# Cutting the last attention unit in two, in a fused attention and gMLP kernel

## The chip, the cores and the metric

The kernel runs on one core of a Trainium2 chip. The metric is the device time of one execution in microseconds (us). TensorE is called PE here, VectorE DVE, ScalarE ACT, GpSimd POOL and SyncE SP, as in the profile.

## What is computed

A gate mixes two branches over the same input x, which has 2048 rows (S) of 512 columns (D), in bfloat16:

```python
g = _sigmoid((x * gate_w).sum(-1, keepdims=True))
# branch A: 32 heads of 16 columns, one shared K and V
q = (x @ wq).reshape(B, S, H, Dh).transpose(0, 2, 1, 3)
k = x @ wk
v = x @ wv
scores = jnp.einsum('bhqd,bkd->bhqk', q, k) * Dh ** (-0.5)
p = _softmax(scores, axis=-1)
o = jnp.einsum('bhqk,bkd->bhqd', p, v)
a = o.transpose(0, 2, 1, 3).reshape(B, S, H * Dh) @ wo
# branch B: gated MLP with a mixing over the sequence
z = _gelu(jnp.einsum('bsd,df->bsf', x, w_in))          # F = 1376, halves of 688
z1 = z[..., :Fh]
z2 = _layernorm(z[..., Fh:], axis=-1)
gg = jnp.einsum('ts,bsf->btf', w_sp, z2) + b_sp[None, :, None]
b = jnp.einsum('bsf,fd->bsd', z1 * gg, w_out)
return g * a + (1 - g) * b
```

## The kernel before

**Units and blocks.** Attention is cut into 32 units (`NU`). Unit u takes four heads and one chunk of 512 queries: c = u // 8 is the chunk, t = (u % 8) // 2 the tile of the Q projection, e = u % 2 one half of its heads. A unit has 64 blocks: 16 tiles of 128 keys times 4 heads. One block is one score product (`s_mm`), 128 keys by 512 queries, into one of the eight PSUM banks of 512 columns; an exponential of it; and one product with V (`o_mm`, called PV), which adds up in one bank (`BO`) for the whole unit, each head in its own 32 rows.

**Two routes for the exponential.** ACT does it with its activation function (`exp_op`, line 770) in steps of two or three banks: even steps own banks 2, 3 and perhaps 4, odd ones banks 0 and 1 (`EB`). DVE and POOL do other blocks by a polynomial, in batches of four (one key tile, four heads): `d_A` (line 782) reads one or two PSUM banks, of banks 5 and 4 (`DBK`), `d_u` (line 789) squares, and `d_w` (line 795, DVE or POOL) squares again. Bank 4 is shared: at each even ACT step the planner decides who has it. Such blocks need two PV products, and each unit with polynomial blocks two constant terms more (`KTV`, `SVB`).

**The end of a unit.** When all its PV products are done, DVE transposes the bank in 32x32 squares (`t1_op`, line 807), `norm_ops` takes the reciprocal of the row sums (line 820), multiplies it with the gate's factor (line 825) and the result with the outputs (line 830), and a second transpose (`t2_op`, line 838) brings them into the form that the output projection reads (`OT`). For the last unit this is done in two halves of 256 queries, interleaved. Only one unit at a time is in the PV bank.

**Outputs.** An output row block (`t2`) is 128 rows. It takes six sets of products with `w_out` (z1*gg) and four with `wo`, one for each pair of units (jp); a set is four 32-column instructions (`fm`). One evacuation scales the sum by the gate, and one DMA stores it. The last unit ends the fourth pair of row blocks 12 to 15. Row blocks 12 and 13 are made in two steps: `g_part` leaves all but the last pair's share in SBUF, `g_fin` adds it. Row blocks 14 and 15 (`g_out`) keep nine of their ten sets waiting in a PSUM bank, and the tenth waits for the last unit. These groups stand in the queue `tails`, in the order: parts 12 and 13, flag, 14, 15, fin 12, fin 13. All four stores are issued by SP, once the flag (a check that the exponentials are in range) is known.

**The order of work.** All of this is planned while the program is built: `build_kernel` simulates PE, ACT and DVE with fixed costs and writes each engine's instructions in the order found. PE takes, in this order: scores for ACT when its banks are free; scores for DVE; rounds of PV; pieces of the fill queues (`first`, `early`, `qs`, `outs`, `main`, `tails`). On the chip each engine follows its own list, and only semaphores tie them. Limits steer the planner, in `PR`:

- `FLEX`: an even ACT step leaves bank 4 to DVE while DVE's planned backlog (ns) is below it.
- `RMIN`: no new polynomial batch is begun in the current unit when fewer blocks (plus 4) are left.
- `PRESS`: PV rounds become urgent when so few of the 19 buffers for exponentials are free.
- `W_MIN`: below this planned share of PE's time, dummy products are put in.

`RLAST` is the same as RMIN for the last unit.

**The start.** x comes in by four transposing DMAs from SP, in the order of chunks 0, 3, 2, 1 (`XO`). While PE waits it runs 12 warm-up products of 128x512 (`WARM`). Then the queue `first` runs: K for the first 128 keys, Q tile 0, the rest of K of chunk 0, V of chunk 0, and so on. The first scores need K for 128 keys and the whole of Q tile 0.

## Time and profile before

| what | value |
|---|---|
| median of three runs | 730.46 us (730.2 to 732.36) |
| profiled execution | 732.71 us |
| its span, first to last instruction | 730.6 us |
| mean granted PE clock | 0.994 |
| busy in the span | PE 712.7, DVE 704.5, ACT 711.4, POOL 467.0 us |
| ACT exponentials (line 770) | 741 instructions with table load, 686.2 us busy |
| score products | 2048 |

A row of the order in time reads: start, length, engine, line, operation, output <- inputs, shape, count, and in brackets the engine's idle time just before and who ended it. Merged instructions stand in one row with the length of the whole. A row of groups reads: line, engine, operation, shapes, count, then busy us and mean ns of one, then the idle time before them. The mean of a pipelined instruction is longer than its distance from the next one. SPq and ACTq are the issue of DMAs on these engines. In rows of stretches the last three columns are the granted PE clock, the share of the DMA engines, and GB/s.

### The profile page before, as it was taken

How to read it: one execution, taken by the hardware profiler on the slowest of the kernel's cores; microseconds unless marked ns; L12 is line 12 of the kernel's file. 1: busy time of each engine (PE TensorE's matmuls, PEld its weight loads, DVE VectorE, ACT ScalarE, POOL GpSimd, SP SyncE). 2: the span in 40 equal slices, each digit the busy share in tenths (PEclk: the TensorE clock that was granted, in tenths of full speed). 3: DMA queues.
4: the chain of work that ended last, by engine and by line, in shares of the span. 5: the costliest groups of instructions: out<-in, count | busy, mean ns of one | idle time of the engine just before them, and what ended most of it. 6: DMA issues, size and time to landing. Idle time of an engine off the chain costs nothing.

```text
span 730.6 us, 21786 instructions
## 1 busy us (share of the span) xinstructions
PE 712.7 (98%) x9037; PEld 208.4 (29%) x9037; DVE 704.5 (96%) x1035; ACT 711.4 (97%) x760; POOL 467.0 (64%) x437
## 2 busy tenths in 40 slices
PE   8999999999999999999999999999999999999995
PEld 3322333323422223222222322222232222222321
DVE  6799999999999999999999999999999999999994
ACT  5999999999999999999999999999999999999994
POOL 5834667661177777776676777767776567668660
PEclk9999999999999999999999999999999999999997
DMA  8341000000000001400000050000005000000001
GB/s 170 125 96 24 2 2 2 1 3 2 2 2 2 1 2 20 99 23 9 2 1 2 3 117 22 10 2 2 2 7 112 15 17 2 2 2 2 2 2 33
DMA packets 48609, 17.29 MB, mean 24 GB/s; under 512 B 44180, under 2 KB 47992, under 8 KB 48504
## 3 DMA queue, kind: packets, MB, share of 16 engines
q1 hardware_dynamic: 46392, 15.67, 9.3%
q8 instruction: 72, 1.18, 0.7%
q10 hardware_dynamic: 2112, 0.17, 0.2%
q14 instruction: 33, 0.27, 0.1%
HBM read 3.25 MB, written 2.10 MB: 7 GB/s over the span
## 4 chain that ended last, share of the span: by engine, by line
PE 71%; ACT 17%; DVE 6%; issue 5%; DMA 1%; ACTq 0%; DVEq 0%
PE ps L354 71%; ACT P L770 16%; DVE UW L782 2%; DVE UW L789 1%; DMA xT<-in_A_x_dram 1%; ACT z L1327 1%; DVE UW L795 1%; DVE bst L598 0%; ACT z L592 0%; DVE km L453 0%; DVE KA L426 0%; DVE T L807 0%; ACT L592 0%; DVE outsb L697 0%; DVE QA L471 0%
## 5 line engine op out<-in xcount | busy, mean ns | idle before, releaser
L770 ACT ACTIVATE P<-ps 128x1024 bf16<-128x1024 f32 (+1 forms) x741 | 686.2, 1182 | 5.9 <-PE ps L354 5.6
L795 POOL TENSOR_TENSOR UW<-UW 128x512 f16<-128x512 f16 (+1 forms) x281 | 363.5, 1294 | 161.2 <-DVE UW L795 67.3
L782 DVE TENSOR_SCALAR UW<-ps 128x512 f16<-128x512 f32 (+1 forms) x424 | 346.1, 837 | 2.5 <-PE ps L354 1.4
L354 PE MATMUL ps<-QA,KA 32*128 32x512 bf16 x2048 | 312.4, 384 | 6.1 <-ACT P L770 2.9
L354 PE MATMUL ps<-P,V 128*32 128x512 bf16 x1496 | 212.4, 385 | 0.4 <-issue 0.2
L354 PEld LDWEIGHTS ps<-QA,KA 32*128 32x128 bf16 x2048 | 84.7, 91 | 308.6 <-ACT P L770 153.5
L789 DVE TENSOR_TENSOR UW<-UW 128x2048 f16<-128x2048 f16 (+1 forms) x163 | 171.4, 1054 | 0.6
L354 PE MATMUL ps<-UW,VW 128*32 128x512 f16 x552 | 118.8, 384 | 0.0
L354 PE MATMUL ps<-wT,z 128*32 128x512 bf16 (+1 forms) x1536 | 116.2, 366 | 0.0
L795 DVE TENSOR_TENSOR UW<-UW 128x1024 f16<-128x1024 f16 (+5 forms) x167 | 108.0, 661 | 0.2
L354 PE MATMUL ps<-UW,V 128*32 128x512 f16 x552 | 84.2, 384 | 0.2 <-DVE T L807 0.2
L354 PEld LDWEIGHTS ps<-P,V 128*32 128x32 bf16 x1496 | 49.1, 94 | 57.4 <-issue 51.6
L475 POOL TENSOR_TENSOR QSQ<-QA 128x512 bf16<-128x512 bf16 x16 | 28.9, 1806 | 22.9 <-DVE z L612 7.0
L354 PEld LDWEIGHTS ps<-wT,z 128*32 128x32 bf16 x1536 | 27.7, 94 | 42.6 <-issue 42.0
L354 PEld LDWEIGHTS ps<-UW,VW 128*32 128x32 bf16 x552 | 28.1, 94 | 14.9 <-issue 11.6
L354 PE MATMUL ps<-wout,z 128*32 128x512 bf16 x384 | 31.6, 384 | 0.0
L354 PE MATMUL ps<-win,xT 128*32 128x344 bf16 x512 | 30.8, 312 | 0.1
L830 POOL TENSOR_TENSOR Tn<-T,rc 128x512 bf16<-128x512 f32 x15 | 24.6, 1639 | 6.4 <-DVE UW L782 3.1
L807 DVE STREAM_TRANSPOSE T<-ps 128x512 f32<-128x512 f32 (+1 forms) x33 | 22.6, 688 | 4.1 <-PE ps L354 4.1
L354 PE MATMUL ps<-QA,KTV 128*32 128x512 bf16 x128 | 25.0, 384 | 0.0
L354 PE MATMUL ps<-CT,SVB 128*32 128x512 bf16 x128 | 24.6, 384 | 0.0
L354 PEld LDWEIGHTS ps<-UW,V 128*32 128x32 bf16 x552 | 19.9, 94 | 15.5 <-issue 11.5
(116 smaller groups left out, 378.5 us busy)
## 6 DMA issues: line engine op xcount, KB each, us to landing
out_dram<-outsb SPq DMA_DIRECT2D x16, 128.0 KB, 1.7
win<-in_B_w_in_dram SPq DMA_DIRECT2D x1, 1376.0 KB, 6.5
wout<-in_B_w_out_dram SPq DMA_DIRECT2D x1, 640.0 KB, 4.2
wo<-in_A_wo_dram SPq DMA_DIRECT2D x8, 64.0 KB, 2.3
UW<-in_A_wq_dram SPq DMA_DIRECT2D x1, 384.0 KB, 3.8
wT<-in_B_w_sp_dram SPq DMA_TRANSPOSE x16, 4.6
UW<-in_A_wq_dram ACTq DMA_DIRECT2D x1, 128.0 KB, 3.9
wout<-in_B_w_out_dram SPq DMA_DIRECT2D x2, 48.0 KB, 1.7
```

What stands on the lines that cost most here:

```text
L354: return t.matmul(dst, lhsT, rhs, start=start, stop=stop, tile_position=tp)
L475: dq(pl_q, 1050.0, lambda: op("pool", lambda v: v.tensor_tensor(QSQ[:, q % 2, :], QA[:, q % NQ, :], QA[:, q % NQ, :], ALU.mult), r=[("Q", ...
L770: op("act", lambda a: a.activation(P[:, 512 * p0:512 * (p0 + n)], ps[:, 512 * b0:512 * (b0 + n)], ACT.Exp), r=[bkey(b0 + i_) for i_ in ran ...
L782: op("dve", lambda v: v.tensor_scalar(UW[:, 0, s, 512 * i:512 * (i + n)], bank(b, 512 * n), Q_A, Q_AS, ALU.mult, ALU.add), r=[bkey(b + j) ...
L789: op("dve", lambda v: v.tensor_tensor(src, src, src, ALU.mult), r=k, w=k, tag="dTT")
L795: op(eng, lambda v: v.tensor_tensor(UW[:, 1, s, 256 * a:256 * b], src, src, ALU.mult), r=[("U", s, h) for h in range(a // 2, (b + 1) // 2) ...
L807: return lambda: pgx.op("dve", lambda v: v.transpose(T1[:, jj, c0:c1], bank(BO, c1 - c0, c0)), r=[bkey(BO)], w=[("T1", jj, c0)], tag="T1")
L830: pgx.op(eng, lambda v: v.tensor_tensor(tnv[:, pr, j0:j1, b0:b1, :], t1v[:, j0:j1, b0:b1, 0:16], rc[:, j0:j1, b0:b1].unsqueeze(3).broadcas ...
L1327: op("act", lambda a: a.activation(z1f[:, 512 * i0:512 * (i0 + n)], ps[:, 512 * b0:512 * (b0 + n)], ACT.Gelu_apprx_tanh), r=[bkey(b0 + j) ...
```

## The change

The last unit of 512 queries becomes two units of 256 (`NB` = 32 before, `NU` = 33 now; `bu(u)` gives the old number). A block of a half-unit is still 512 columns wide: two neighbouring key tiles of 256 queries each (`kts`), so it takes two score products and two PV products for each one before, each 256 columns wide. A half-unit has 32 blocks, and each has its own transpose, normalisation and back-transpose. The score products of a step are collected and written out together (`s_flush`). `RHALF` and `max` limit the polynomial batches of the half-units.

Row blocks 12 and 13 need only the first half's result. Their `g_fin` groups now use bank 7 (`BM`) and stand ahead of 14 and 15 in `tails`, so their evacuations and stores come during the second half. Row block 14 is evacuated and stored by ACT, 15 by DVE and SP.

At the start, Q tile 0 is made and evacuated in halves (`g_Q0`), into two banks. PE holds the first scores' place when Q tile 0 is due before the next piece would end (`HSL`). The 12 warm-up products of 512 columns become 43 of 128, and their operand's first 128 columns are set first. The memset of `KTV` goes from DVE to POOL, and small DVE instructions are put ahead of the ones that wait for wq. The planner's assumed arrival times change, and it doubles the cost of a head piece before its time 7000 (`COLD`).

While the last unit's PV is on, DVE leaves itself free for a transpose that is due within 150 ns (`TCH`). Four limits change.

```diff
-NU = 32
+NB = 32
+NU = 33
-WARM = 12
+WARM = 43
 RLAST = 16
+RHALF = 16
+TCH = 1
+TBM = True
+COLD = 7000.0
+HSL = 30.0
-PR = dict(... PRESS=5, FLEX=5000.0, RMIN=32, WBL=0.5, W_MIN=0.9, ...)
+PR = dict(... PRESS=6, FLEX=3800.0, RMIN=36, WBL=0.5, W_MIN=0.92, ...)
...
-        op("dve", lambda v: v.memset(CT[:], 1.0 / 64.0), w=["CT"])
+        op("dve", lambda v: v.memset(CT[:, 0:128], 1.0 / 64.0), w=["CT0"])
+        op("dve", lambda v: v.memset(CT[:, 128:512], 1.0 / 64.0), w=["CT"])
...
-        op("dve", lambda v: v.memset(KTV[:], 0.0), w=["KTV"])
...
+        op("pool", lambda v: v.memset(KTV[:], 0.0), w=["KTV"])
...
-            mm(bank(0), CT[:, 0:128], CT[:], True, True, ["CT"], [bkey(0)], tag="warm")
+            mm(bank(0, 128), CT[:, 0:128], CT[:, 0:128], True, True, ["CT0"], [bkey(0)], tag="warm")
...
+        def g_Q0(h, b):
+            def piece(dt):
+                return lambda: fm(b, 256, 0, wqd[:, dt, 0, :], xT[:, dt, 512 * XO[0] + 256 * h:512 * XO[0] + 256 * h + 256], dt == 0, dt == 3,
+                                  ["wqd0"] + xk(XO[0], 256 * h, 256 * h + 256), "Q")
+            def ev():
+                op("dve", lambda v: v.tensor_copy(QA[:, 0, 256 * h:256 * h + 256], bank(b, 256)), r=[bkey(b)], w=[("Q", 0)], tag="Qev")
...
+        def bu(u):
+            return min(u, NB - 1)
+        def kts(u, kt):
+            return (kt,) if u < NB - 1 else (2 * kt, 2 * kt + 1)
...
+        def s_flush():
+            for i in range(2):
+                for b, (u, k, g), key in s_pend:
+                    ks = kts(u, k)
+                    if i >= len(ks):
+                        continue
+                    kt, w = ks[i], 512 // len(ks)
+                    e, q, q0 = bu(u) % 2, (bu(u) // 2) % NQ, 0 if u < NB - 1 else 256 * (u - NB + 1)
+                    kr = ["K0a" if kt == 4 * XO[0] else ("K0", kt // 4)] if e == 0 else [("K1", kt // 4)]
+                    mm(bank(b, w, w * i), KA[32 * g:32 * g + 32, e, 128 * kt:128 * kt + 128], QA[32 * g:32 * g + 32, q, q0:q0 + w], True, True,
+                       kr + [("Q", q)], [key], tp=(32 * g, 0), chan="s", tag="S")
+            s_pend.clear()
...
-            if u == NU - 1:
-                for h in range(2):
-                    dq(t1_q, 370.0, t1_op(pg, u, 256 * h, 256 * h + 256), t, None)
...
+            if u >= NB - 1:
+                h = u - NB + 1
+                dq(t1_q, 370.0, t1_op(pg, u, 256 * h, 256 * h + 256), t, setT(("O", u)))
+                for z in norm_ops(pg, c, jp, [1], 8 * h, 8 * h + 8, [("T1", 1, 256 * h)]):
+                    dq(t1_q, *z, t, None)
+                rk = [("Tn", pr, 0, 0), ("Tn", pr, 1, 8 * h)]
+                dq(t1_q, 370.0, t2_op(pg, c, jp, 256 * h, 256 * h + 256, rk, ("OT", 3, 3, h)), t, setT(("OT", 3, 3, h)))
                 return
...
-        first = deque([g_K(XO[0], 0, 128), g_Q(0, DBK[0]), g_K(XO[0], 128, 512), g_V(XO[0], BO), ...
+        first = deque([g_K(XO[0], 0, 128), g_Q0(0, DBK[0]), g_Q0(1, BO), g_K(XO[0], 128, 512), g_V(XO[0], DBK[0]), ...
...
-        tails = deque([g_part(12), g_part(13), g_flag(),
-                       g_out(14, BM, None, True, "sp"),
-                       g_out(15, DBK[0], lambda: d_done(), True, "sp"),
-                       g_fin(12, EB[0][0], lambda: when(("Bend", 0)), "sp"),
-                       g_fin(13, EB[1][0], lambda: when(("Bend", 1)), "sp")])
+        tail_f = [g_fin(12 + i, BM if TBM else EB[i][0], (lambda: 0.0) if TBM else (lambda i=i: when(("Bend", i))), "sp") for i in range(2)]
+        tail_o = [g_out(14, BM, None, True, "act"), g_out(15, DBK[0], lambda: d_done(), False, "sp")]
+        tails = deque([g_part(12), g_part(13), g_flag()] + (tail_f + tail_o if TBM else tail_o + tail_f))
...
+                c_ = fp[1].pieces[fp[1].pos][0] * (2.0 if now < COLD else 1.0)
+                q0 = T.get(("Q", 0), 0.0)
+                if k == 0 and now < q0 < c_p + c_ - HSL:
+                    return None
...
+            if t1_q and st_["pu"] >= NU - TCH and qt(t1_q[0]) <= now + 150.0:
+                return None
```

## The prediction

> **What bounds the kernel now.** I read the busy shares of the page first, then busy time by stretches, then the groups with shapes kept apart, then the order of time in the first 10 and the last 15 us.

> ```profile
> PE 712.7 (98%) x9037; PEld 208.4 (29%) x9037; DVE 704.5 (96%) x1035; ACT 711.4 (97%) x760; POOL 467.0 (64%) x437
> 600.00:700.00 100.00, 100.00 (x1225) 28.27 (x1223) 99.22 (x134) 100.00 (x110) 70.30 (x60) 1.00 0.01 3
> 710.00:720.00 10.00, 9.78 (x128) 2.86 (x128) 6.07 (x10) 9.43 (x9) 1.46 (x2) 1.00 0.01 2
> ```

> (The columns of the second and third rows are the stretch, its length, then busy us of PE, PEld, DVE, ACT and POOL.) In the body three engines are full at once: 99 to 100 of 100 us. ACT does 110 steps in 100 us, 0.909 us a step. So the body gets shorter only if the split of blocks between ACT and DVE gets better, not by removing a wait. The slack lies at the ends: DVE falls to 6.07 of 10 us before the last exponential has ended, and behind it comes a serial tail.

> ```profile
> 704.08 15.35 ACT L770 ACTIVATE P<-ps 128x1024 bf16<-128x1024 f32 x15
> ...
> 719.48 0.39 PE L354 MATMUL ps<-P,V 128*32 128x512 bf16 x2
> 719.92 0.78 DVE L807 STREAM_TRANSPOSE T<-ps 128x256 f32<-128x256 f32 x2 [3.90 <-PE ps L354]
> ...
> 721.46 0.76 DVE L838 STREAM_TRANSPOSE OT<-Tn 128x256 bf16<-128x256 bf16 x2
> 721.95 1.90 PE L354 MATMUL ps<-wo,OT 128*32 128x512 bf16 x16 [2.07 <-DVE OT L838]
> ...
> 722.62 1.41 DVE L697 SCALAR_TENSOR_TENSOR outsb<-ps,G,z 128x512 bf16<-128x512 f32 x2 [0.40 <-PE ps L354]
> ...
> 723.40 3.18 SPq L662 DMA_DIRECT2D out_dram<-outsb  x4
> 723.47 1.27 ACT L728 ACTIVATE outsb<-ps,G 128x512 bf16<-128x512 f32 x2 [4.04 <-PE ps L354]
> ```
> ```profile
> 724.18 2.39 SPq L662 DMA_DIRECT2D out_dram<-outsb  x3
> ```
> ```profile
> L662 SPq DMA_DIRECT2D out_dram<-outsb x16: 332/338/1202, 311.2 to 726.1; - x16
> ```

> The last exponential ends at 704.08 + 15.35 = 719.43. Then: last products 719.48, transposes, normalisation, back-transposes to 722.22, sixteen products of the output projection, two evacuations on DVE and two on ACT, four stores on one queue, the last of which is issued at 726.1. The span ends at 730.6, 4.5 us behind that issue: 11.2 us with hardly any overlap.

> At the head ACT waits until 9.27:

> ```profile
> 1.44 4.45 PE L353 MATMUL ps<-CT 128*128 128x512 bf16 x12 [1.44 <-DVE CT L254]
> ...
> 6.37 0.41 PE L354 MATMUL ps<-xT,wk_rep 128*32 128x128 bf16 x16 [0.48 <-DMA xT<-in_A_x_dram]
> ...
> 6.59 1.05 PE L354 MATMUL ps<-xT,wqd 128*32 128x512 bf16 x16
> ...
> 7.14 0.29 DVE L426 CAST KA<-ps 128x128 bf16<-128x128 f32 x1 [1.05 <-PE ps L354]
> ...
> 7.69 0.69 DVE L471 CAST QA<-ps 128x512 bf16<-128x512 f32 x1 [0.26 <-PE ps L354]
> ...
> 8.14 0.71 PE L354 MATMUL ps<-wvg,xT 128*32 128x33 bf16 x56
> ...
> 8.78 0.39 PE L354 MATMUL ps<-QA,KA 32*128 32x512 bf16 x4
> ...
> 9.27 5.28 ACT L770 ACTIVATE P<-ps 128x1536 bf16<-128x1536 f32 x5 [5.01 <-PE ps L354]
> ```

> Q is in SBUF at 7.69 + 0.69 = 8.38, but the first scores start at 8.78, since the V products stand before them in PE's order.

> **The tail, costed.** The second half-unit has one transpose, one chain of normalisation and one back-transpose where the pair of halves has two of each:

> ```profile
> L807 DVE STREAM_TRANSPOSE T<-ps 128x256 f32<-128x256 f32 x2 | 0.8, 429 | 3.9 <-PE ps L354 3.9
> L838 DVE STREAM_TRANSPOSE OT<-Tn 128x256 bf16<-128x256 bf16 x2 | 0.8, 419 | 0.0
> L830 DVE TENSOR_TENSOR Tn<-T,rc 128x128 bf16<-128x128 f32 x2 | 0.5, 284 | 0.0
> L820 DVE RECIPROCAL rc<-T 128x8 f32<-128x8 f32 x2 | 0.3, 182 | 0.0
> L825 DVE TENSOR_TENSOR rc<-rc,RT 128x8 f32<-128x8 f32 x2 | 0.3, 148 | 0.0
> ```

> Single durations 429 + 182 + 148 + 284 + 419 ns = 1.46 us. The pair interleaves and hides the hand-off between dependent instructions; a single chain shows it, so I add 0.2 (estimate): T2 ends at 719.92 + 1.66 = 721.6, not 722.22. Then two sets of products instead of four, 721.65 to about 722.4, and two evacuations at once: ACT's (0.69, half of the 1.27 with its start) to 722.9, DVE's (about 0.75) to 723.15. One store goes out on ACT's queue, one on SP's. SP's second store was issued 0.15 after its evacuation (722.62 + 1.41 = 724.03, then 724.18), so its issue now stands at about 723.3 in place of 726.1: **-2.8 us**. In the group rows the longest issue took 1202 ns against a median of 338; if the pair meets that, 0.9 comes back. If the last stores also land sooner because two share the engines instead of four, some 0.3 more is gained. Bounds -3.1 to -1.9.

> The clock has a part in it:

> ```profile
> 722.00:723.00 1.00, 1.00 (x12) 0.41 (x16) 0.60 (x2) 0.00 (x0) 0.00 (x0) 0.50 0.00 0
> ```

> The granted clock is 0.50 there, some two us after PE fell idle. In the changed kernel output products can fill that pause (below), and the last sets then run at full clock; that is in the 722.4.
> [...]

> **What is moved ahead.** Row blocks 12 and 13 need only the first half-unit: two sets of products, two DVE evacuations (1.41 together) and two SP stores now run while the second half computes, as does the first half's chain of 1.46. DVE has room: it stood idle 3.90 us before the final transpose. SP must have seen the flag before its first store; the flag is made ahead of these groups, and nothing else is queued on SP. ACT's store is the last thing on ACT.

> The price is on PE. The groups come from one queue in order, so the nine early sets each of row blocks 14 and 15 now wait until 12 and 13 have begun. Before, they ran here:

> ```profile
> 706.00:708.00 2.00, 0.88 (x12) 0.22 (x12) 0.00 (x0) 1.00 0.00 0
> ...
> 714.00:716.00 2.00, 0.97 (x16) 0.23 (x12) 0.00 (x0) 1.00 0.00 0
> ```

> ```profile
> 712.88 0.39 PE L354 MATMUL ps<-wout,z 128*32 128x512 bf16 x4
> ...
> 713.53 0.61 PE L354 MATMUL ps<-wout,z 128*32 128x512 bf16 x8
> ```

> (First the stretches of PE products that read wout, first and last; then two rows of the order in time.) A set of four takes 0.39 us alone and 0.61 - 0.39 = 0.22 behind another, so 18 sets are 3.9 us. They can start about 5 us before the last exponential ends: the second half has 32 blocks, of which ACT does some 20 (estimate), ten steps or 9 us, and the first half's chain and two BM evacuations take about 4 of them. In those 5 us PE gives perhaps 0.33 us a step, 1.9; the pause after the last PV gives another 1.7. That holds nearly all; I charge **+0.2**, bounds 0 and +1.9 (nine sets uncovered).

> **Cutting the unit.** Scores and PV of its 64 blocks come as 256-wide instructions, twice as many:

> ```profile
> L354 PE MATMUL ps<-wT,z 128*32 128x512 bf16 x1280 | 105.2, 384 | 0.0
> ...
> L354 PE MATMUL ps<-wT,z 128*32 128x256 bf16 x256 | 11.0, 276 | 0.0
> ```

> The 512-wide product takes 384 ns, the 256-wide one 276: 256 columns cost 108, no fixed part shows, so about **+0.1**. One more hand-over of the single PV bank holds PV back for one half transpose, 0.43 and a wait: covered by other products, 0; uncovered it is one ACT step, +0.9.

> **The head.** The Q tile in halves lets DVE start earlier, though two 256-wide evacuations together take more than 0.69; Q is ready at about 8.2 to 8.4. What moves is the order: PE now waits for Q and issues the scores before the V pieces, 8.35 instead of 8.78. **-0.4** for ACT's first step. It is worth nothing if DVE or PE set the next 20 us, -0.6 if all lines up. Warm-up:

> ```profile
> L353 PEld LDWEIGHTS ps<-CT x12: 98/151/151, 1.4 to 5.3; 128*128 128x128 bf16 x12
> ```

> Twelve 512-wide products took 4.45 us from 1.44. Forty-three quarter-wide ones have 43/48 of those columns, 4.0 us, and start some 0.3 earlier: over by 5.2, 1.2 us before x. Were the weight load (151 ns) to pace them, 43 x 0.151 = 6.5 us, ending at 7.6, 1.2 us late. Value 0, bounds 0 and +1.2.
> [...] No run here shows 128-wide warm-ups.

> The KTV memset goes from DVE to POOL:

> ```profile
> 13.07 0.95 POOL L340 MEMSET bspz<- 128x1024 bf16 x1
> ...
> 19.11 0.53 POOL L509 TENSOR_SCALAR VW<-V 128x128 bf16<-128x128 bf16 x1 [1.89 <-DVE gs L495]
> ```

> Twice 1024 elements, so 1.9 us ahead of bspz, and POOL stands idle 1.89 us before 19.11: absorbed, 0. Uncovered, KTV comes up to 1.9 later.

> **The limits.** They reorder everything between. Costs of the two routes:

> ```profile
> L770 ACT ACTIVATE P<-ps 128x1024 bf16<-128x1024 f32 x725 | 668.1, 1175 | 0.5 <-PE ps L354 0.3
> L782 DVE TENSOR_SCALAR UW<-ps 128x512 f16<-128x512 f32 x296 | 191.1, 676 | 1.9 <-PE ps L354 1.2
> L782 DVE TENSOR_SCALAR UW<-ps 128x1024 f16<-128x1024 f32 x128 | 155.0, 1211 | 0.6 <-PE ps L354 0.2
> ```

> A block on ACT costs 0.909/2 = 0.45 us; a DVE batch of four spares ACT 1.8. The 296 + 2 x 128 = 552 blocks are 138 batches. FLEX at 3800 leaves the shared bank to ACT more often, RMIN at 36 stops late batches, PRESS at 6 issues PV rounds sooner, W_MIN adds dummy products. Two batches more would be -3.6, three fewer +5.4. DVE was full in the body before, so no term has a clear sign: value 0, both ends kept.

> Sum: -2.8 + 0.2 + 0.1 - 0.4 = **-2.9**. The profiled execution took 732.71 (span 730.6 and 2.1 around it); the sum would make it 729.8. It stands 2.25 above the median 730.46, so a median is forecast at **727.5**.

> **Rivals.**
> 1. The limits help too: one or two DVE batches more, -1.8 to -3.6 on top: 724 to 725.7. For it: the last fifteen steps took 15.35/15 = 1.02 us against 0.909, 1.7 us lost. Against: DVE is full. 0.25.
> 2. The gain is taken back on PE: 18 sets late (+1.9) or a late warm-up (+1.2): 728.7 to 729.4, no change. 0.15.
> 3. Slower: FLEX takes the shared bank from DVE and its paired first steps break up. A pair costs 1211 ns, two singles 1352, so 141 ns each. With DVE full, its loss is spread over both engines: DVE does 552 of 2048 blocks, 27%, so end time grows by about 0.27 of it, 0.04 a pair; all 128 pairs cost 4.9. Alone it offsets 2.9 only from 76 pairs on, but each DVE batch that the bank no longer feeds adds up to 1.8; with three batches fewer (+5.4): 727.5 + 5.4 = 732.9. 0.12.
> 4. The change does not do what it says: the first half's stores stay at the end, because unit 31's PV is closed only when ACT is nearly done. Then only the head's 0.4 and ACT's own queue are left: 729.5. 0.05.

> My forecast holds 0.43. About 0.3%, 2.2 us, is what a measurement can tell from no change: faster means below 728.3. From the cases: faster 0.68 (forecast and rival 1), same 0.2 (rivals 2 and 4), slower 0.12 (rival 3). The range takes rival 1's far end and rival 3's near one: 723.3 to 732.5; the likeliest case's own range is 726 to 729.

> **What would show it.** Two output stores some 8 us ahead of the end, on SP, and two last ones on two queues less than 4 us after the last PV; the first exponential at about 8.9; the last at about 719; 138 batches give or take two, read from the count of 128x512 products of UW and VW (552); the 18 sets between 714 and 722. Wrong would be a changed count of ACT steps that outweighs the tail, PE products between the last PV and T2 that run past it, or warm-ups that end after x has landed.

## The result, and the profile after

The changed kernel took **732.71 us** (median of 18 runs, 730.72 to 734.48) against 730.32 for the kernel before (18 runs, 729.89 to 732.94): ratio **1.0025, 95% interval 1.0016 to 1.0034**. By the medians it is slower by 2.4 us (the ratio compares the means: 1.8 us), where 3 us less were forecast.

The profiled execution of after took 732.71 us too, with a span of 730.9. The shown execution of before was one of its longer ones, so a second profile of the unchanged kernel was taken (730.16 us, span 728.2, granted clock 0.997), and all comparisons below are with that. First the page's busy line of after, then two stretches of each kernel (columns as in the prediction: stretch, length, busy us of PE, PEld, DVE, ACT, POOL, granted clock, DMA share, GB/s).

```profile
PE 715.8 (98%) x9304; PEld 215.4 (29%) x9304; DVE 704.4 (96%) x1041; ACT 711.1 (97%) x757; POOL 471.8 (65%) x442
```

Kernel before, second profile:

```profile
10.00:30.00 20.00, 18.89 (x440) 7.05 (x428) 14.51 (x32) 19.94 (x22) 14.87 (x31) 1.00 0.60 148
30.00:700.00 670.00, 664.11 (x8213) 191.39 (x8209) 665.08 (x948) 669.02 (x718) 440.28 (x377) 1.00 0.08 18
```

After:

```profile
10.00:30.00 20.00, 17.42 (x384) 6.06 (x380) 12.99 (x25) 16.35 (x17) 13.73 (x26) 0.83 0.65 142
30.00:700.00 670.00, 664.49 (x8304) 191.85 (x8304) 663.29 (x959) 669.53 (x717) 446.99 (x387) 1.00 0.09 18
```

ACT's work is the same (711.1 us against 711.4). The loss is in the first 30 us: ACT was busy 16.35 of 20 us in place of 19.94, and PE's mean clock there was 0.83. The body is full in both (669.53 and 669.02 of 670).

ACT in order of time in that stretch, after:

```profile
9.04 1.94 ACT L811 ACTIVATE P<-ps 128x1536 bf16<-128x1536 f32 x2 [4.77 <-PE ps L363]
12.76 3.28 ACT L811 ACTIVATE P<-ps 128x1536 bf16<-128x1536 f32 x3 [1.78 <-PE ps L363]
16.45 1.02 ACT L811 ACTIVATE P<-ps 128x1024 bf16<-128x1024 f32 x1 [0.41 <-PE ps L363]
18.03 1.02 ACT L811 ACTIVATE P<-ps 128x1024 bf16<-128x1024 f32 x1 [0.56 <-PE ps L363]
19.49 1.02 ACT L811 ACTIVATE P<-ps 128x1024 bf16<-128x1024 f32 x1 [0.43 <-PE ps L363]
20.98 9.63 ACT L811 ACTIVATE P<-ps 128x1024 bf16<-128x1024 f32 x9 [0.47 <-PE ps L363]
```

The first step comes at 9.04, in before's second profile at 9.74: 0.70 won. After two steps ACT waits 1.78 us for scores, then about 0.47 ahead of each of the four rows until 20.98: 1.78 + 0.41 + 0.56 + 0.43 + 0.47 = 3.65 us idle. What PE did meanwhile, in order of time, after:

```profile
1.04 4.77 PE L362 MATMUL ps<-CT 128*128 128x128 bf16 x43 [1.04 <-DVE CT L260]
6.22 0.62 PE L363 MATMUL ps<-xT,wk_rep 128*32 128x128 bf16 x16 [0.41 <-DMA xT<-in_A_x_dram]
6.60 1.27 PE L363 MATMUL ps<-xT,wqd 128*32 128x256 bf16 x32
7.70 0.83 PE L363 MATMUL ps<-xT,wk_rep 128*32 128x384 bf16 x16
8.35 0.27 PE L363 MATMUL ps<-wvg,xT 128*32 128x33 bf16 x16
8.55 0.39 PE L363 MATMUL ps<-QA,KA 32*128 32x512 bf16 x4
8.88 0.54 PE L363 MATMUL ps<-wvg,xT 128*32 128x33 bf16 x48
9.31 1.05 PE L363 MATMUL ps<-xT,wk_rep 128*32 128x512 bf16 x16
10.17 0.46 PE L363 MATMUL ps<-wvg,xT 128*32 128x33 bf16 x31
12.07 0.27 PE L363 MATMUL ps<-wvg,xT 128*32 128x33 bf16 x13 [1.44 <-issue]
```

The warm-ups end at 5.81, before x. Then, in the middle of a run of 44 equal V products, PE stops for 1.44 us with no operand late ("issue": nothing the profile shows was waited for). The counts ahead of the stop add up to 43+16+32+16+16+4+48+16+31 = **222 products**. Before the kernel is over its clock, too, has halved twice; stretches of 3.41 us and what follows them, after:

```profile
10.45:13.86 3.41, 1.65 (x55) 0.70 (x41) 1.16 (x2) 1.63 (x3) 1.72 (x5) 1.00 0.79 157
13.86:20.70 6.84, 6.56 (x45) 1.18 (x45) 4.67 (x10) 5.25 (x6) 6.18 (x10) 0.50 0.81 144
713.61:717.02 3.41, 2.54 (x42) 0.86 (x42) 3.38 (x6) 3.41 (x5) 0.00 (x0) 1.00 0.06 19
717.02:720.42 3.40, 3.40 (x40) 0.96 (x42) 3.40 (x6) 3.14 (x3) 0.00 (x0) 0.50 0.19 65
```

From 13.86 to 20.70 PE is full at half clock and ACT waits for it. The tail, after:

```profile
716.00 11.26 SPq L686 DMA_DIRECT2D out_dram<-outsb  x3
...
719.09 1.45 ACT L811 ACTIVATE P<-ps 128x1536 bf16<-128x1536 f32 x1 [0.26 <-PE ps L363]
...
720.81 1.02 ACT L811 ACTIVATE P<-ps 128x1024 bf16<-128x1024 f32 x1 [0.27 <-PE ps L363]
...
722.11 1.02 ACT L811 ACTIVATE P<-ps 128x1024 bf16<-128x1024 f32 x1 [0.28 <-PE ps L363]
...
723.95 0.45 DVE L849 STREAM_TRANSPOSE T<-ps 128x256 f32<-128x256 f32 x1 [2.71 <-PE ps L363]
...
726.37 0.69 ACT L752 ACTIVATE outsb<-ps,G 128x512 bf16<-128x512 f32 x1 [3.24 <-PE ps L363]
727.09 0.37 ACTq L686 DMA_DIRECT2D out_dram<-outsb  x1
```

Kernel before, second profile:

```profile
717.59 2.05 ACT L770 ACTIVATE P<-ps 128x1024 bf16<-128x1024 f32 x2
...
720.13 0.78 DVE L807 STREAM_TRANSPOSE T<-ps 128x256 f32<-128x256 f32 x2 [3.89 <-PE ps L354]
...
722.16 1.05 PE L354 MATMUL ps<-wo,OT 128*32 128x512 bf16 x16 [2.07 <-DVE OT L838]
...
723.04 1.26 ACT L728 ACTIVATE outsb<-ps,G 128x512 bf16<-128x512 f32 x2 [3.40 <-PE ps L354]
```

Here is a surprise about the forecast's own base. The unchanged kernel's tail, from the last exponential's end (719.64) to the span's end (728.2), is **8.5 us** in this execution, and 11.2 in the one that was shown. There the sixteen output products had taken 1.90 us at half clock (here 1.05), and from the last evacuation's end to the span's end it was 730.6 - 724.74 = 5.9 us (here 728.2 - 724.30 = 3.9). After's tail is 730.9 - 723.13 = 7.8. The whole difference of the two spans, +2.7 us, step by step (after minus before's second profile):

| step | before | after | difference |
|---|---|---|---|
| first exponential | 9.74 | 9.04 | -0.70 |
| ACT idle from there to 30 us | 0.06 | 3.65 | +3.59 |
| ACT idle, 30 to 700 us (670 less busy) | 0.98 | 0.47 | -0.51 |
| ACT idle, 700 us to the last exponential | 0 | 0.26+0.27+0.28 = 0.81 | +0.81 |
| ACT's own work up to the last exponential (rest) | | | +0.30 |
| last exponential's end to the last transpose | 0.49 | 0.82 | +0.33 |
| transpose to the last evacuation's end | 4.17 | 3.11 | -1.06 |
| last evacuation's end to the span's end | 3.90 | 3.84 | -0.06 |
| sum | | | +2.70 |

### The profile page after: what moved, and what is told of

The parts are those of the page before. It is cut to its first block, busy times and chain, and to the rows that moved or that the text cites. A ratio compares the mean times of both kernels' runs of the same rounds, so it can differ in the third digit from the quotient of the medians.

```text
span 730.9 us, 22335 instructions
## 1 busy us (share of the span) xinstructions
PE 715.8 (98%) x9304; PEld 215.4 (29%) x9304; DVE 704.4 (96%) x1041; ACT 711.1 (97%) x757; POOL 471.8 (65%) x442
## 4 chain that ended last, share of the span: by engine, by line
PE 69%; ACT 18%; DVE 8%; issue 4%; DMA 1%; ACTq 0%
PE ps L363 69%; ACT P L811 17%; DVE UW L824 3%; DVE bst L622 2%; DVE UW L831 1%; DMA xT<-in_A_x_dram 1%; DVE UW L837 1%; ACT z L616 0%; DVE KA L435 0%; DVE mv L626 0%; DVE QA L480 0%; ACT L616 0%; DVE T L849 0%; ACTq L161 0%; ACT outsb L752 0%
## 5 line engine op out<-in xcount | busy, mean ns | idle before, releaser
L363 PE MATMUL ps<-QA,KA 32*128 32x512 bf16 (+1 forms) x2112 | 312.2, 379 | 7.0 <-ACT P L811 3.9
L363 PE MATMUL ps<-P,V 128*32 128x512 bf16 (+1 forms) x1540 | 207.3, 381 | 0.0
L363 PE MATMUL ps<-UW,VW 128*32 128x512 f16 (+1 forms) x572 | 119.3, 376 | 0.0
L837 DVE TENSOR_TENSOR UW<-UW 128x1024 f16<-128x1024 f16 (+4 forms) x174 | 107.6, 633 | 0.1
L363 PE MATMUL ps<-UW,V 128*32 128x512 f16 (+1 forms) x572 | 82.2, 379 | 0.0
L484 POOL TENSOR_TENSOR QSQ<-QA 128x512 bf16<-128x512 bf16 x15 | 26.0, 1736 | 9.9 <-DVE UW L837 4.4
L363 PE MATMUL ps<-CT,SVB 128*32 128x512 bf16 (+1 forms) x132 | 24.4, 378 | 0.0
L363 PE MATMUL ps<-QA,KTV 128*32 128x512 bf16 (+1 forms) x132 | 24.0, 377 | 0.0
```

Source lines behind the costliest of these rows:

```text
L363: return t.matmul(dst, lhsT, rhs, start=start, stop=stop, tile_position=tp)
L484: dq(pl_q, 1050.0, lambda: op("pool", lambda v: v.tensor_tensor(QSQ[:, q % 2, :], QA[:, q % NQ, :], QA[:, q % NQ, :], ALU.mult), r=[("Q", ...
L837: op(eng, lambda v: v.tensor_tensor(UW[:, 1, s, 256 * a:256 * b], src, src, ALU.mult), r=[("U", s, h) for h in range(a // 2, (b + 1) // 2) ...
```

## The experiments

Theory A, a guess formed from the stop behind the 222nd product (1.44 us, no operand late) and from the half clock behind it (13.86 to 20.70): PE's instructions come in portions, and the new start uses up a portion before the next has arrived; the idle time then costs the clock. Rivals: B, the warm-ups' shape or their end costs (too cold, too late); C, the four limits made a worse plan; D, the cut of the last unit costs more than it brings.

**1. The old warm-ups in the new kernel.** 12 products of 512 columns.

```diff
-WARM = 43
+WARM = 12
-            mm(bank(0, 128), CT[:, 0:128], CT[:, 0:128], ...)
+            mm(bank(0), CT[:, 0:128], CT[:], ...)
```

> The changed kernel with the old warm-up alone: 12 products of 128x512 and their operand set at once; every other instruction and its order as in the changed kernel. Theory A (PE's instruction stream stalls at its 222nd product, which the 43 small warm-ups and the split Q tile bring too early): the stall of 1.44 us at 10.63 comes 31 products later, behind the first V products of chunk 3, and is shorter; the granted clock stays near 1.0 between 10 and 20 us in place of 0.69; ACT has 9 or more busy us there in place of 6.8; the time is 2 to 4 us below the changed kernel, 728.5 to 730.5. Theory B (the new limits cost the time): no change beyond 0.5 us, 732. Theory C (the end of the kernel costs it, by a clock that falls at 717): no change in the head, 732.

731.9 us (731.14 to 732.99, 8 runs; before 730.16), ratio 1.0027 [1.0016, 1.0037]: above the 728.5 to 730.5 that theory A had expected. PE in order of time around the stop:

```profile
11.27 0.20 PE L362 MATMUL ps<-wvg,xT 128*32 128x33 bf16 x4
13.25 0.23 PE L362 MATMUL ps<-wvg,xT 128*32 128x33 bf16 x8 [1.77 <-issue]
```

The stop has moved to 11.5, other products stand ahead of it, and their count is again 12+16+32+16+16+4+48+16+44+3+8+3+4 = 222. Fewer warm-ups alone don't remove it.

**2. Count against shape.** 10 large warm-ups, then 33 products of one column: 43 instructions, with the warming done by large ones.

```diff
-        for _ in range(WARM):
-            mm(bank(0, 128), CT[:, 0:128], CT[:, 0:128], ...)
+        for _ in range(10):
+            mm(bank(0), CT[:, 0:128], CT[:], ...)
+        for _ in range(33):
+            mm(ps[0:1, 0:1], CT[:, 0:1], CT[:, 0:1], ...)
```

> The changed kernel with 10 warm-up products of 128x512 and 33 of a single column: as many products as the 43, but the warming done by large ones. Theory A: the stall stands at the same product, the 222nd, and the time stays at 732 to 733.5. Rival D (not the count but the small products' weaker warming lets the clock fall): the clock holds through 10 to 20 us and the time falls to 729 to 730.5 as with the old warm-up.

732.74 us (730.24 to 735.56, 12 runs), ratio 1.0035 [1.002, 1.0051]: as slow as after. The stop, 1.90 us, again ends ahead of the 223rd product, at 12.94. The shape of the warm-ups (B) falls as the cause; the number of instructions matters. These warm-ups end at 6.8, later than the 5.81 of after, and the first step comes at 9.45; an end that is too late is answered by after itself, where the warm-ups end 0.41 us before the first products on x.

**3. The many warm-ups in the kernel before.** Nothing else changed but their operand, whose first 128 columns are set first.

```diff
-WARM = 12
+WARM = 43
-            mm(bank(0), CT[:, 0:128], CT[:], ...)
+            mm(bank(0, 128), CT[:, 0:128], CT[:, 0:128], ...)
```

> The kernel before with the new warm-up alone: 43 products of 128x128, the first 128 columns of their operand set first; all else as before. Theory A: its 222nd product comes 31 products earlier, among the V products of chunk 3 or the K products ahead of them; a stall of 1 us or more stands at 10 to 12 us where 0.68 us stood at 13.4; the granted clock falls in the 10 us behind it in some or all executions; 731.5 to 734. Theory B and C: 730.3, within 0.5.

733.64 us (731.84 to 734.09, 5 runs), ratio 1.0039 [1.0026, 1.0052]: this line of the change by itself loses 3.5 us.

```profile
14.04 0.35 PE L355 MATMUL ps<-wvg,xT 128*32 128x33 bf16 x22 [1.69 <-issue]
```

The kernel before has its own small stop of 0.57 us ahead of the 223rd product (start to start, at 14.04), nearly all covered by work that ACT has; 31 more instructions ahead of it make it 1.69.

**4. A quarter of the instructions.** K, V and the first Q tile of the start are written as four 32-column products each. Here each four are one 128-column product with the same result; with 12 large warm-ups, all else as in after.

```diff
+        def fw(b, n, off, lhsT, rhs, start, stop, r, tag):
+            mm(ps[:, 512 * b + off:512 * b + off + n], lhsT, rhs, start, stop, r, [bkey(b)], tag=tag)
...
-                return lambda: fm(b, 256, 0, wqd[:, dt, 0, :], ...
+                return lambda: fw(b, 256, 0, wqd[:, dt, 0, :], ...
```

(and the same in `g_K` and `g_V`)

> The changed kernel with 12 large warm-ups, and the K, V and first Q products of the start as one 128-column product each in place of four of 32 columns: the same sums in the same order with a quarter of PE's instructions there. Theory A: PE reaches its 222nd product past 18 us instead of 11.5, the stall is gone or falls where it is covered, the clock holds, the first step comes at 8.6 or earlier, and the time is 726 to 728.5. If the single products cost more than the stall (weight loads of 128 columns, or a change of tiling between them and the score products): 730 or above.

**728.77 us** (727.82 to 733.59, 12 runs; before 730.28, 23 runs), ratio 0.999 [0.9973, 1.0007]. ACT in order of time, then 20 us of the stretches:

```profile
9.01 17.56 ACT L813 ACTIVATE P<-ps 128x1536 bf16<-128x1536 f32 x17 [4.75 <-PE ps L362]
```
```profile
10.00:30.00 20.00, 18.84 (x256) 6.74 (x254) 14.18 (x31) 19.89 (x22) 17.30 (x35) 1.00 0.53 143
```

Seventeen exponentials run on end, with no stop; PE issues 256 products in these 20 us in place of before's 440. The profiled execution has a span of 726.7. Eight of the twelve runs took 727.8 to 729.0 at a granted clock of 0.997 or more, four 730.2 to 733.6 at 0.988 to 0.994. So with the start mended the rest of the change seems worth about 1.5 us where the clock holds. Over all twelve runs no gain is shown: the interval holds 1.

**5. The same in the kernel before.** K and V of the start wide.

> The kernel before with its K and V products of the start as one 128-column product each in place of four. Theory A: its stall of 0.6 us goes, ACT's idle time to 30 us was only 0.3 us, so at most 0.5 us is gained: 729.5 to 730.3. If wide products cost by themselves: 731 or above, and the same amount has to be taken off the result of the changed kernel with wide products.

732.97 us (730.72 to 734.37, 12 runs), ratio 1.0028 [1.0016, 1.0041]: worse, although no stop is left. (About 1 us of it lies outside the span: in the median run the time exceeds the span by 3 us here and by 2 in the kernel before.)

```profile
9.65:13.06 3.41, 2.50 (x29) 0.94 (x26) 1.38 (x7) 3.35 (x4) 2.54 (x7) 1.00 1.13 238
13.06:19.88 6.82, 6.82 (x36) 1.08 (x33) 4.71 (x7) 5.58 (x6) 3.54 (x7) 0.50 0.75 233
```

PE was busy 2.50 of 3.41 us from 9.65 on, and the clock halved for 6.82 us behind it. So the clock halved here without the stop, as it did in after behind a stretch of 3.41 us in which PE was busy 1.65: of theory A, this run shows the second half without the first.

**6. Only K and Q wide.** V stays in four, to keep PE busier; 12 large warm-ups.

> The changed kernel with 12 large warm-up products, and with the K and first-Q products of the start as one 128-column product each; V stays in four 32-column products. Theory A (PE's instructions arrive late at a fixed count, the 222nd): K and Q lose 3 of 4 instructions, so the count is reached about 1.5 us later than in the run with large warm-ups alone (13.25) but earlier than with V wide too; the pause is shorter than 1 us, and more of it is covered by work that ACT already has; time 728 to 730. Theory B (the wide products make PE idle more and so lose the clock): V in four keeps PE busier between 8 and 20 us, the clock holds in more executions than with all three wide, and the time is 727.5 to 728.5. Rival (neither, only the number of warm-up instructions counts): as with 12 large warm-ups alone, 731.9.

732.42 us (730.22 to 735.2, 12 runs; before 730.45), ratio 1.0024 [1.0011, 1.0038]. I expected 727.5 to 730; the miss shows most. No stop at the 222nd product, which comes only at 16.7. But later, PE in order of time and then ACT:

```profile
20.27 0.59 PE L362 MATMUL ps<-V,KN 128*32 128x32 bf16 x56
22.37 0.22 PE L362 MATMUL ps<-V,KN 128*32 128x32 bf16 x4 [1.51 <-issue]
```
```profile
23.62 1.02 ACT L813 ACTIVATE P<-ps 128x1024 bf16<-128x1024 f32 x1 [1.47 <-PE ps L362]
```

A stop of 1.51 us, ahead of the 348th product (counted in the trace), 125 behind the 223rd, inside another run of small products. The clock had halved at 21.42 already, inside the stop, behind a stretch (18.01 to 21.42) in which PE was busy 2.43 of 3.41 us, and it stayed so until 28.24. So the 222nd product is no oddity of its place: a stop of the same kind, 1.51 us with no operand late, stands some 125 products behind it too.

**7. Every product of that kind wide, through the whole kernel.**

> The changed kernel with 12 large warm-up products and with every full-width product (K, V, Q, PV, output projection) of the whole kernel as one 128-column instruction instead of four of 32 columns: a quarter of the instructions for these through the whole span. Theory A (instruction supply matters at the start alone): the head as with K, V and Q wide, no pause at the 222nd product; in the body nothing changes, since PE is bound by columns there: 727.5 to 729.5. Theory C (fewer instructions free PE's sequencer in the body as well): below 727. Rival D (four 32-column products run side by side on PE's column groups and hand over without a gap, one wide product does not, or the clock falls): 731 or more, with PE's idle time in the body above that of the kernel before.

737.28 us (735.05 to 740.05, 6 runs), ratio 1.0099 [1.0072, 1.0125]. The head is as in 4 (first exponential 8.70, no idle to 26 us), so the loss lies behind:

```profile
710.00:720.00 10.00, 8.28 (x145) 3.37 (x141) 8.91 (x15) 9.90 (x11) 1.66 (x2) 0.89 0.05 16
```

PE paused (8.28 of 10), the mean clock fell to 0.89, and the last exponential ended at 726.8. The row holds little of the loss: ACT was idle for 2.35 us between 30 and 700 us and 2.38 from 700 us to the last exponential (0.82 and 0 in experiment 4), and its own work up to there took 713.3 us in place of 708.7. Why was not taken apart. A quarter of the instructions helped at the start alone (728.77 us in experiment 4).

**8. The limits.** The four old limits in the changed kernel:

```diff
-PRESS=6, FLEX=3800.0, RMIN=36, WBL=0.5, W_MIN=0.92
+PRESS=5, FLEX=5000.0, RMIN=32, WBL=0.5, W_MIN=0.9
```

> The changed kernel with the four old limits. Theory A: the head is planned nearly the same, the stall and the low clock stay, 731 to 733. Theory B: the time falls by 2 us or more, below 730.5.

736.9 us (733.71 to 737.34, 6 runs), ratio 1.0083 [1.0068, 1.0098], which neither theory had expected. The reverse, the four new limits alone in the kernel before:

> The kernel before with the four new limits alone. The changed kernel lost 4.2 us when they were set back, so if they are better by themselves: 726 to 729. If they only suit the cut unit or the new start (the planner's order changes as a whole with each): 730 to 734.

735.2 us (734.83 to 737.66, 6 runs), ratio 1.0071 [1.0056, 1.0086]. C falls as a cause of the loss, and the limits are no gain of their own either: +4.9 us in the kernel before, -4.2 in the changed one.

**9. The whole old start** (order, warm-ups, Q in one piece, memsets) with the cut unit and the new limits:

```diff
-        first = deque([g_K(XO[0], 0, 128), g_Q0(0, DBK[0]), g_Q0(1, BO), g_K(XO[0], 128, 512), ...
+        first = deque([g_K(XO[0], 0, 128), g_Q(0, DBK[0]), g_K(XO[0], 128, 512), ...
-COLD = 7000.0
-HSL = 30.0
+COLD = 0.0
+HSL = 1e9
...
```

> The changed kernel with the whole start as before: 12 large warm-ups, one Q tile, the old places of the memsets and small DVE instructions, the old assumed times. The cut unit, its early stores and the new limits stay. Theory A (the start costs what the end gains): stall of about 0.6 us at the 222nd product, ACT idle below 1 us from its first step to 30 us, first step at 9.3, last at about 719.5, then 7.8 us: a span of 725 to 727.5 and a time of 727 to 729, faster than before by 0.2 to 0.45%. Theory B (the new limits or the cut cost it): 730 or above even so.

738.42 us (736.55 to 739.2, 4 runs), ratio 1.0113 [1.0099, 1.0128]: a wide miss. Order of time:

```profile
712.67 0.43 DVE L848 STREAM_TRANSPOSE T<-ps 128x256 f32<-128x256 f32 x1
...
720.69 0.74 DVE L707 TENSOR_SCALAR z<-ps,G 128x512 f32<-128x512 f32 x1
721.85 0.45 DVE L848 STREAM_TRANSPOSE T<-ps 128x256 f32<-128x256 f32 x1 [0.41 <-PE ps L362]
...
723.47 0.10 DVE L777 CAST flag<-ps 1x1 int32<-1x1 f32 x1
...
724.86 6.95 SPq L685 DMA_DIRECT2D out_dram<-outsb  x3
```

The first half's transpose is as early as in after (712.67; 712.48 there), and the second half's comes 0.9 us behind the last exponential (720.95). What is late is the queue `tails`: the part of row block 13 is evacuated only at 720.69 (709.21 in after) and the flag is known only at 723.47 (714.08 in after). All that stands behind it in the queue comes then, the first half's stores too, and the last evacuation starts at 730.70. The stores stay at the end, as in the prediction's rival 4, but not for the reason that it gave (a late end of the first half). Why PE left these pieces so late under the new limits is not shown.

**10. The cut alone:** 9 with the old limits as well.

> The cut of the last unit and the early stores alone: the start and the four limits are those of the kernel before, so only the tail's part of the change is left (the order of the whole kernel is still planned anew). Theory A (the tail's step is a gain by itself, the rest of the loss came from the start): last exponential to end 7.8 to 8.6 us, the last exponential at 718.5 to 719.7 as before, 47 blocks begun by 30 us, time 726.5 to 728. Theory B (every new plan costs, unless its limits are chosen for it): the last exponential ends at 721 or later, or unit 31 closes late and the distance to the end is 13 us, as in the run with the start of before and the new limits (738.42): 732 to 739. Theory C (the tail gives nothing by itself): 730 to 731.

730.82 us (median of 10 runs; nine took 730.33 to 733.04, one 1949.23), before 730.07, ratio 1.001 [0.9999, 1.0021]. Order of time:

```profile
719.91 0.69 DVE L836 TENSOR_TENSOR UW<-UW 128x1024 f16<-128x1024 f16 x1
...
721.10 0.45 DVE L848 STREAM_TRANSPOSE T<-ps 128x256 f32<-128x256 f32 x1 [0.49 <-PE ps L362]
...
723.69 0.69 ACT L751 ACTIVATE outsb<-ps,G 128x512 bf16<-128x512 f32 x1 [4.41 <-PE ps L362]
```

The stores of row blocks 12 and 13 are early, transpose to last evacuation takes 724.38 - 721.10 = 3.28 us in place of 4.17, and the clock holds to the end (1.0 over the span). But the last exponential ended at 719.28 and the transpose waits until 721.10 for a DVE batch that is multiplied until 720.60: 1.8 us in place of 0.5. The gain is eaten by the late batch. Here, then, it is the place of the last batch that is late; in 9 it was the output pieces. (D: no loss of its own is shown, and no gain.)

The runs with the start and the limits set apart, medians:

| | old limits | new limits |
|---|---|---|
| start of before, unit whole | 730.3 | 735.2 |
| start of before, unit cut | 730.8 | 738.4 |
| new start, unit cut | 736.9 | 732.7 |
| new start with wide products, unit cut | | 728.8 |

**11. The kernel before again**, for the second profile used above.

> The kernel before, unchanged, for a second profile of it. Theory (the shown profile was one of its longer executions, its body is the same each time): span 727.6 to 729 at a granted clock of about 0.997, the 222nd product of PE again behind a pause of 0.5 to 0.7 us that ends at 14.0 +- 0.2, and a distance from the last exponential's end to the span's end below 11.2, by up to 2 us, since less of it runs at half clock. Rival (the longer time came from the body): the last exponential ends 2 us earlier than 719.4 and the tail stays at 11.2.

730.16 us, span 728.2; last exponential at 719.64, tail 8.5, half clock in its last 4.3 us. The rival falls: the body was the same, the shown execution's excess lay in the tail, 2.2 us of it behind the issue of the last store.

## Why the prediction was wrong

**The head, -0.4: the step that failed.** The prediction ordered PE's products by their operands alone: "PE now waits for Q and issues the scores before the V pieces, 8.35 instead of 8.78. -0.4 for ACT's first step". That much came true: scores at 8.55, and the first step 0.70 earlier than in the second profile of the kernel before (0.23 earlier than in the shown one). What it did not ask is whether PE can stop with no operand late, as it did for 1.44 us in after. In the kernel before, the small stop stood in the order of time of the shown execution:

```profile
14.04 0.39 PE L354 MATMUL ps<-P,V 128*32 128x512 bf16 x2 [0.19 <-issue]
...
14.82 9.70 ACT L770 ACTIVATE P<-ps 128x1024 bf16<-128x1024 f32 x10 [0.27 <-PE ps L354]
```

The 223rd product starts here, and ACT waits 0.27 us behind it: a sign that was passed over. The new start sends products faster: 43 warm-ups for 12, 32 Q products for 16, and small V products early. The price was 3.59 us of ACT idle time, 1.78 in the stop and 0.41 to 0.56 ahead of each of four steps at half clock. Bounds of -0.6 to 0 held nothing of it.

**Warm-up, 0, bounds 0 and +1.2.** The forecast "over by 5.2, 1.2 us before x" had the side of x right: they ended at 5.81, 0.41 before the first products on x (6.22). They took 4.77 us, not 4.0, which cost nothing. The sixteen first K products took 0.62 us, 0.41 in the shown execution of the kernel before. But its second profile has 0.59 there, and the changed kernel with the old limits (experiment 8), with the same 43 warm-ups, 0.41; so this differs between executions and not by the warm-ups alone. The cost, 3.5 us by itself in the kernel before (experiment 3), went with the count of instructions (experiment 2: as many of another shape, 732.74 us), for which the sum had no term.

**The tail, -2.8: the last issue moved nearly as forecast, the end did not follow it as far.** The stores of row blocks 12 and 13 did go out in the second half (SP's first at 716.00), the 18 sets did fit, T1 to the end of T2 took 725.65 - 723.95 = 1.70 us for a forecast 1.66. "Its issue now stands at about 723.3 in place of 726.1" is 3.9 us behind the last exponential in place of 6.7; after has 727.09 - 723.13 = 4.0. In before's second profile it is 725.9 - 719.6 = 6.2 (the row gives shortest, median and longest issue in ns, then the first and last start):

```profile
L662 SPq DMA_DIRECT2D out_dram<-outsb x4: 332/430/1586, 723.4 to 725.9; - x4
```

But from the last issue to the span's end it is 4.5 us in the shown execution, 2.3 in the second, and 3.8 in after; the last store lands 4.0, 1.8 and 2.9 us behind its issue. The forecast kept the 4.5 and then took off 2.25 as that execution's excess over the median, so it left only 2.2 for this stretch. Of the 2.0 us that the tail fell short of the forecast, 1.5 lie here. The other 0.5 was counted twice: the shown execution issued its last store 0.5 later than the second, and both the -2.8 and the 2.25 took that off. What sets the landing is not shown: from issue to landing ACT's last store took 2.7 to 3.6 us in eight of the nine profiles with the cut unit (1.7 in experiment 9), the last store 4.0 and 1.8 in the two of the kernel before.

**18 sets, +0.2, and the cut, +0.1:** ACT's own work grew by 0.30 in all. That is the sum of the two terms, but nothing shows that it comes from them: in experiment 2, with the same plan behind the start, it is 708.9 us, as in the kernel before (709.2 in after). In the stretch from 713.61 PE paused 0.87 us and the clock halved for 3.4 us, and ACT then waited 0.81: not foreseen. In experiment 2 PE was busy 2.54 of 3.41 us in the same stretch, the clock held (1.00 there and to 720.42), and ACT waited for nothing. The hand-over of the PV bank shows no step of its own.

**Limits, 0, -3.6 to +5.4:** as a term of its own it measured +4.9 in the kernel before and -4.2 in the changed one. DVE's share did not move (552 blocks before; 532 at 512 columns and 40 at 256 after, which is 552). So no batch was won or lost. What the limits moved in the profiles is the end: the output pieces in experiment 9 and in the second kernel of experiment 8 (flag at 723.52 there, 706.50 in before's second profile), the last batch in experiment 10. Three of the four plans that mix old and new cost 4 to 8 us more than the one that they are compared with; the fourth, the cut alone, cost nothing clear. Zero came true by luck: the sum had nothing that ties the limits to the plan.

**KTV memset, 0:** no wait for it is seen; right.

By the terms: forecast -2.9. Measured: first step and stop +2.89, tail -0.79, idle time in the body and the last 20 us +0.30, own work +0.30, together +2.7. Of the 5.6 us between, 3.3 are the stop and the clock behind it, 2.0 the tail.

Of the rivals none was it. Rival 2 had PE take the gain back, but by late sets or a late warm-up, and only to no change. The outcome, slower, was given 0.12 under another mechanism (rival 3, broken pairs), which the trace denies: pairs rose from 128 to 133. No rival had PE stop in the first 30 us. The ends of the range, 723.3 and 732.5, are not the figures of the rivals that it names (724 and 732.9).

## What to carry to other kernels

Count instructions as well as columns where an engine starts: here PE stopped for 1.44 us in a run of small products, behind 222 products and with no operand late, and the profile before had an "issue" wait of 0.19 us at the same count. Such a row is worth a count of the products ahead of it. A gain at the end is counted up to the landing of the last store, not up to its issue: take a second profile first, since that last stretch differed by 2.2 us between two executions of one kernel. When a planner is rerun, its limits and its plan belong together; test an edit with the limits refitted too.

## What the runs showed of the hardware

**The instruction queue moved 16.4 KB a packet, and PE stopped behind 222 products.** Page of before's second profile, DMA queues (packets, MB, share), and a 1 us stretch of after, 9.5 to 10.5:

```profile
q8 instruction: 72, 1.18, 0.7%
```
```profile
q8 instruction: 1, 0.02, 6.2%
```

1.18 MB in 72 packets is 16.4 KB each. 9037 products with as many weight loads are 18,074 instructions, so a packet would hold 251, or some 126 products, if the queue carried these alone (an estimate). The stops stood behind 222 products in every kernel that had one there and behind 347 in experiment 6, some 125 further on. In after such a transfer starts at 9.82 us and the 223rd product at 12.07; in experiment 1 it is 10.96 and 13.25, in experiment 2 10.66 and 12.94, in the shown execution of before 11.60 and 14.04. So in these four the product behind the stop began 2.3 to 2.4 us behind the start of a transfer, each time with x still coming in. That the product waited for this transfer is the author's reading of the times and was not tried by itself. The 222 products ahead of it were through by 10.63 in after, and PE stopped for 1.44; in the shown execution of before the 222nd began at 13.47, and the stop was 0.57. What sets the start of the transfer was not tried.
